# A fused linear-attention and MLP kernel: w_in products of batch 0 ahead of the last normalisation column, with the loads behind them reordered

## The chip, the cores and the metric

The kernel runs on one core of a Trainium2 chip. The metric is the device time of that core in microseconds, the median of several executions. The profile's span is mostly about 1.8 us shorter than that time. "Column c" below means one of the four 128-row slices of the MLP's input x.

Differences of a few tenths are therefore read in the profiles, and medians are only the check.

## The reference

Eight batches of 8 heads, 576 positions, head size 64. Each head's keys and values make a 64x64 matrix, the queries are multiplied by it, and the result is normalised over the head's 64 values. The heads side by side are the rows of an MLP with an ELU between its two matrices.

```python
kv  = np.einsum('bhsd,bhse->bhde', k, v)
out = np.einsum('bhsd,bhde->bhse', q, kv)
rms = np.sqrt(np.mean(out * out, axis=-1, keepdims=True) + 1e-06)
x   = (out / rms * g_norm).transpose(0, 2, 1, 3).reshape(4608, 512)
h   = x @ w_in                                   # 512 x 2048
g   = np.where(h > 0, h, np.exp(np.minimum(h, 0)) - 1)
return g @ w_out                                 # 2048 x 512
```

Inputs and output are fp32; the kernel multiplies in bf16.

## The kernel before

The work goes in nine groups of 512 rows: the first 512 positions of each batch, then one group of all the remainders. TensorE alternates between group T's w_in products (`mm1`), group T-1's w_out products (`mm2`) and the attention of T+1. Only the start differs: nothing has been loaded yet. Batch 0's attention is done with x transposed from the outset, one column c at a time, and TensorE is kept busy with products of zeros (`idle`).

```python
    packed_kv(0)
    for c in range(4):
        fetch_packed_kv("k", 0, slice(c, c + 1))
        # ...
        fetch_packed_kv("v", 0, slice(c, c + 1))
    for s in range(4):
        load_w_in(s)                    # 512 columns each, fp32 to bf16 on the way
    fetch_packed_q(1)
    packed_kv(1)
    for name in "kv":
        fetch_packed_kv(name, 1, slice(0, 2))
    load_w_out(0)                       # four of sixteen row blocks
    for name in "kv":
        fetch_packed_kv(name, 1, slice(2, 4))
    # ...
    fetch_q(0)                          # sync queue, two DMAs
    # ...
    exp_first(2)
    square_first(3, V)                  # copy and multiply on VectorE
    scale_first(1)
    scale_first(2)
    mean0[3] = bank(3)
    idle(idle_ps, 5)
    mean_first(3)
    log_first(3)
    exp_first(3)
    scale_first(3)                      # last column of x
    head.close()
    # ... PSUM pools: ps_at one tile of two banks, ps_m1 two such tiles, ps_m2 two banks
    for c in range(KC):                 # 16 products: tiles 0 to 3, column by column
        for f in (2, 3, 0, 1) if c == 0 else range(4):
            nc.tensor.matmul(firsts[f // 2][:, f % 2, :],
                lhsT=w_in_sb[:, c, f * P : f * P + P], rhs=x0[:, c, :],
                start=(c == 0), stop=(c == KC - 1))
    # ...
    for i in range(2):
        elu(0, i, [(0, 2, firsts[i])], i == 0)()
    for i in range(2, 8):
        mm1(0, i, relu=i in (2, 4, 7), spare=i in (3, 6))()
        if i in (3, 5):
            load_w_out(i // 2)
        if i == 5:
            at["q"]()                   # transposes of batch 1's Q
    # ... w_out 12 to 15, batch 2's loads ...
    at["kv0"]()                         # K1/V1 product, first half of the heads
    # ...
    for j in order:
        mm2_quarter(0, j, 0)            # w_out blocks 0 to 3
    at["kv1"]()
    at["se"]({0: None, 1: wide})        # Q1 times KV1, then squares, sums, scales
    # ...
    for j in order:
        mm2_quarter(0, j, 1)            # needs w_out blocks 4 to 7
    # ... blocks 8 to 15, with batch 1's x transposes x0 and x1 between them
```

Of the kernel before, what the change touches and what calls it, by code (L numbers as in the profile page):

```python
# [8 lines left out]
FP32 = mybir.dt.float32  # L9
# [7 lines left out]
def kernel(  # L17
# [117 lines left out]
    def load_w_in(s):  # L135
        cols = slice(s * 512, s * 512 + 512)
        nc.gpsimd.dma_start(  # L137
            out=w_in_sb[:, :, cols], in_=moe_w_in.rearrange("(c p) f -> p c f", p=P)[:, :, cols]
        )

    def load_w_out(s):
        fs = slice(4 * s, 4 * s + 4)
        nc.gpsimd.dma_start(
            out=w_out_sb[:, fs, :], in_=moe_w_out.rearrange("(c p) f -> p c f", p=P)[:, fs, :]
        )
# [7 lines left out]
    def q_tile(b):  # L153
        bf["q", b] = qkvp.tile([P, J, H, D], BF16, name="q_bf", tag="q")
        st = raw.pop(("q", b))
        if b < B:
            return st.rearrange("p (h j d) -> p j h d", h=H, j=J)
# [27 lines left out]
    def q_t_single(q_pk, qt_ps, p):  # L185
        for j in range(J):
            for l in range(2):
                nc.tensor.transpose(
                    qt_ps[l * 64 : l * 64 + 64, p, j * P : j * P + P],
# [3 lines left out]

    def q_t_mm(q_sb, qt_ps, p):
        for j in range(J):
            nc.tensor.transpose(
                qt_ps[:, p, j * P : j * P + P],
                q_sb[:, j, 2 * p : 2 * p + 2, :],
                ident,
            )  # L200
# [50 lines left out]
    def attention(T):  # L251
        st = {}

        def q_t():
# [3 lines left out]
            for p in range(NPAIR):  # L258
                q_t_single(raw["q", T], qt_ps, p)
# [130 lines left out]
    def mm1(T, i, cols=(slice(0, 512),), relu=False, spare=False, between=()):  # L390
# [4 lines left out]
        if spare:  # L395
            h_ps = [ps_m2.tile([P, G], FP32, name="h_ps", tag="mm2") for _ in range(2)]
            parts = [(a, a + 1, h_ps[a].rearrange("p (a t) -> p a t", a=1)) for a in range(2)]
        else:
            both = ps_m1.tile([P, 2, G], FP32, name="h_ps", tag="mm1")
# [91 lines left out]

    packed_kv(0)
# [5 lines left out]
    for s in range(4):  # L498
        load_w_in(s)
    fetch_packed_q(1)  # L500
    packed_kv(1)
    for name in "kv":
        fetch_packed_kv(name, 1, slice(0, 2))
    load_w_out(0)
# [11 lines left out]
    fetch_q(0)  # L516
# [14 lines left out]
    def idle(ps, n):  # L531
        for _ in range(n):
            nc.tensor.matmul(ps, lhsT=zeros[:, 0:P], rhs=zeros, start=True, stop=True)

    kv_ps = ps_head.tile([P, 2, G], FP32, name="kv_ps", tag="kv")
    idle_ps, qt_b, g_ps = bank(0), bank(1), bank(2)
    mean0 = {1: bank(3)}
    qt_ps = [
        t.bitcast(BF16).rearrange("p (r t) -> p r t", r=2) for t in (bank(4), bank(5), qt_b)
    ]  # L540
    idle(idle_ps, 9)
    q_st = q_tile(0)
    qT0 = attp.tile([P, NPAIR, G], BF16, name="qT", tag="qT")

    def q_cast(p, eng):
        hs = slice(2 * p, 2 * p + 2)
        copy_on(eng, bf["q", 0][:, :, hs, :], q_st[:, :, hs, :])

    for p, eng in ((0, V), (1, A)):
        q_cast(p, eng)  # L550
        q_t_mm(bf["q", 0], qt_ps[0], p)
    nc.vector.tensor_copy(out=qT0[:, 0:2, :], in_=qt_ps[0])
    idle(idle_ps, 2)
    for p, eng in ((2, V), (3, A)):
        q_cast(p, eng)
# [25 lines left out]
    def square_first(c, eng):  # L581
        if eng is A:
            nc.scalar.activation(sq0[c], se0[c], AF.Square)
        else:
            nc.vector.tensor_copy(out=r0[c], in_=se0[c])
            nc.vector.tensor_tensor(out=sq0[c], in0=r0[c], in1=se0[c], op=ALU.mult)
# [15 lines left out]
    q_t_mm(bf["q", 0][:, :, 4:8, :], qt_ps[1], 0)  # L602
    nc.vector.tensor_copy(out=qT0[:, 2, :], in_=qt_ps[1][:, 0, :])
    kv_first(0)
    q_t_mm(bf["q", 0][:, :, 4:8, :], qt_ps[2], 1)
    nc.scalar.copy(qT0[:, 3, :], qt_ps[2][:, 1, :])
# [8 lines left out]
    se0 = {c: bank(c) for c in range(2)}  # L615
    se_first(0)
    square_first(0, A)
    kv_first(1)
    idle_ps = bank(4)
    mean0[0] = bank(2)  # L620
    mean_first(0)
    log_first(0)
    se_first(1)
    square_first(1, A)
    exp_first(0)
    idle(idle_ps, 1)
    kv_first(2)
    idle(idle_ps, 1)
    mean_first(1)
    scale_first(0)  # L630
    for c in range(2, 4):
        se0[c] = bank(2 + c)
    se_first(2)
    square_first(2, A)
    log_first(1)
    exp_first(1)
    kv_first(3)
    idle_ps = bank(2)
# [227 lines left out]
```

## Time and profile before

| | before |
|---|---|
| median time | 285.86 us (3 runs), 285.78 with the three runs taken beside the changed kernel |
| span of the profile | 283.9 us |
| TensorE busy | 97% |
| first w_in product | 15.34 us |
| first product of batch 1 | 47.69 us |

The head of the page of the kernel before: span, the busy time of the engines with their shares of the span, and from the second part the rows of 40 equal slices (7.1 us each).

```profile
span 283.9 us, 5147 instructions
PE 274.1 (97%) x2115; PEld 129.6 (46%) x2145; DVE 161.2 (57%) x235; ACT 152.8 (54%) x217; POOL 53.1 (19%) x93
...
PE   7899999999999999999999999999999999999994
...
DMA  7999999797993596356953794355233123010122
GB/s 193 204 207 202 206 203 178 224 167 135 177 173 57 150 158 158 74 144 82 194 122 113 111 195 104 101 132 157 39 92 94 77 39 99 10 76 0 75 74 74
```

TensorE is the bound, and the loads run flat out for the first six slices, to about 43 us. Busy time of pipelined matmuls overstates, so the better reading is the distance between starts: a 128x512 product starts 0.216 us after the one ahead of it (eight take 1.73 us).

Next, lines of the timeline of TensorE of the kernel before. Columns: start in us, us until the last of the merged instructions ends, engine, line, operation, output<-inputs, partitions x elements, count, and in brackets the idle time ahead and what ended it. L533 are products of zeros, L589 and L665 the last mean and the first w_in products; L177, L212 and L453 are the K1/V1 product, Q1 times KV1, and the w_out products; L406 at the end is batch 1's first.

```profile
13.76 1.24 PE L533 MATMUL bank<-zeros 128*128 128x512 bf16 x5
15.12 0.39 PE L589 MATMUL bank<-sq,means 128*128 128x512 bf16 x1
15.34 0.38 PE L665 MATMUL at<-xT,w_in_sb 128*128 128x512 bf16 x1
...
30.37 0.48 PE L177 MATMUL at<-v_pk,k_pk 64*64 64x64 bf16 x36
31.01 3.63 PE L453 MATMUL o_ps<-w_out_sb,gT 128*128 128x512 bf16 x15 [0.17 <-DMA w_out_sb<-in_moe_w_out_dram]
34.57 0.48 PE L177 MATMUL at<-v_pk,k_pk 64*64 64x64 bf16 x36
35.43 0.41 PE L212 MATMUL at<-kv_sb,qT 64*128 64x64 bf16 x16 [0.38 <-ACT kv_sb L363]
...
36.44 5.34 PE L453 MATMUL o_ps<-w_out_sb,gT 128*128 128x512 bf16 x23 [0.37 <-DMA w_out_sb<-in_moe_w_out_dram]
...
47.69 2.54 PE L406 MATMUL h_ps<-xT,w_in_sb 128*128 128x512 bf16 x11
```

Three holes stand here: after the first K1/V1 product (0.64 us from start to start), after the second (0.86) and after Q1 times KV1 (1.01). Two of them end with a w_out load.

When a load lands can be read from GpSimd, whose queue lets it issue a new DMA only when an older one has landed. Lines of GpSimd's timeline of the kernel before:

```profile
14.85 0.74 POOL L143 DMA_DIRECT2D w_out_sb<-in_moe_w_out_dram  x1 [1.66 <-DMA w_in_sb<-in_moe_w_in_dram]
18.07 0.70 POOL L118 DMA_DIRECT2D k_pk<-in_k_dram  x1 [2.48 <-DMA w_in_sb<-in_moe_w_in_dram]
20.57 0.71 POOL L118 DMA_DIRECT2D v_pk<-in_v_dram  x1 [1.80 <-DMA w_in_sb<-in_moe_w_in_dram]
23.11 0.74 POOL L143 DMA_DIRECT2D w_out_sb<-in_moe_w_out_dram  x1 [1.83 <-DMA w_in_sb<-in_moe_w_in_dram]
```

The four w_in slices landed about 0.3 us ahead of these starts: 14.6, 17.8, 20.3 and 22.8 us.

### The profile page before, as it was taken

The numbers are of one execution on the slowest core, as the hardware profiler recorded it, in microseconds if no ns is written. First come the engines' busy times: TensorE is split into PE (matmuls) and PEld (weight loads), VectorE is DVE, ScalarE is ACT, GpSimd is POOL, SyncE is SP. The second block draws the span as 40 slices with busy tenths as digits, with TensorE's granted clock in tenths as the row PEclk, the third lists the DMA queues.
The fourth block names the chain that finished last, engine by engine and source line by source line (L and its number), as shares of the span: only waits on it lengthen the run. The fifth ranks groups of instructions, "written<-read, shape, count | busy, mean of one in ns | idle before, by whom it ended". The sixth has DMA issues, their size and how long they took to land.

```text
span 283.9 us, 5147 instructions
## 1 busy us (share of the span) xinstructions
PE 274.1 (97%) x2115; PEld 129.6 (46%) x2145; DVE 161.2 (57%) x235; ACT 152.8 (54%) x217; POOL 53.1 (19%) x93
## 2 busy tenths in 40 slices
PE   7899999999999999999999999999999999999994
PEld 2444454445444444444444444444444444444444
DVE  2458561779378646934694458544864486444400
ACT  2779544766496337633773378246923692333311
POOL 7834302341431241004210421002000000000000
PEclk9999999999999999999999999999999999999999
DMA  7999999797993596356953794355233123010122
GB/s 193 204 207 202 206 203 178 224 167 135 177 173 57 150 158 158 74 144 82 194 122 113 111 195 104 101 132 157 39 92 94 77 39 99 10 76 0 75 74 74
DMA packets 55963, 35.98 MB, mean 127 GB/s; under 512 B 32772, under 2 KB 53508, under 8 KB 55940
## 3 DMA queue, kind: packets, MB, share of 16 engines
q0 software_dynamic: 20192, 17.30, 39.7%
q1 hardware_dynamic: 35348, 17.83, 23.2%
q10 hardware_dynamic: 400, 0.52, 0.6%
q8 instruction: 16, 0.26, 0.4%
q14 instruction: 7, 0.06, 0.1%
HBM read 36.70 MB, written 9.44 MB: 163 GB/s over the span
## 4 chain that ended last, share of the span: by engine, by line
PE 80%; DMA 11%; DVE 4%; issue 1%; ACT 1%; POOL 1%; DVEq 0%; POOLq 0%
PE h_ps L406 36%; PE o_ps L453 36%; PE o_ps L825 5%; DMA w_in_sb<-in_moe_w_in_dram 5%; DMA w_out_sb<-in_moe_w_out_dram 5%; DMA k_pk<-in_k_dram 2%; PE at L177 1%; DVE gT L437 1%; DVE xs L240 1%; DVE ss L229 1%; POOL w_in_sb L137 1%; PE at L212 1%; PE se_ps L212 1%; DVE elu_e L429 0%; PE at L316 0%
## 5 line engine op out<-in xcount | busy, mean ns | idle before, releaser
L406 PE MATMUL h_ps<-xT,w_in_sb 128*128 128x512 bf16 x556 | 130.7, 379 | 0.3
L453 PE MATMUL o_ps<-w_out_sb,gT 128*128 128x512 bf16 x489 | 117.9, 379 | 1.8 <-DMA w_out_sb<-in_moe_w_out_dram 0.5
L418 ACT ACTIVATE elu_e<-h_ps 128x1024 bf16<-128x1024 f32 (+1 forms) x75 | 73.1, 982 | 82.6 <-PE h_ps L406 81.0
L406 PEld LDWEIGHTS <-w_in_sb 128*128 128x128 bf16 x560 | 53.2, 98 | 64.5 <-DVE xT L344 1.7
L453 PEld LDWEIGHTS <-gT 128*128 128x128 bf16 x512 | 49.8, 98 | 59.5 <-issue 0.3
L429 DVE TENSOR_SCALAR elu_e<-elu_e 128x1024 bf16<-128x1024 bf16 (+1 forms) x76 | 32.3, 425 | 75.4 <-ACT elu_e L418 75.4
L437 DVE TENSOR_TENSOR gT<-elu_e,h_ps 128x1024 bf16<-128x1024 bf16 (+1 forms) x56 | 64.1, 1145 | 5.8
L466 ACT COPY o_sb<-o_ps 128x512 f32<-128x512 f32 x32 | 18.5, 586 | 17.4 <-PE o_ps L453 17.4
L229 DVE TENSOR_REDUCE ss<-sq 128x16 f32<-128x1024 bf16 x16 | 19.3, 1217 | 7.7 <-ACT sq L224 6.9
L151 POOL COPY q_bf<-q_pk 128x512 bf16<-128x512 bf16 x24 | 14.9, 648 | 26.3 <-DMA q_pk<-in_q_dram 22.6
L424 ACT ACTIVATE elu_h<-h_ps 128x1024 bf16<-128x1024 f32 x19 | 19.3, 1015 | 0.0
L437 DVE TENSOR_TENSOR gT<-elu_e,elu_h 128x1024 bf16<-128x1024 bf16 x19 | 13.5, 713 | 3.6 <-ACT elu_h L424 2.4
L825 PE MATMUL o_ps<-w_out_sb,gT 128*128 128x512 bf16 (+1 forms) x79 | 14.0, 336 | 0.1
L125 POOL COPY gate<-qT 1x1 bf16<-1x1 bf16 x6 | 1.1, 179 | 61.5 <-DMA qT<-q_bf 61.5
L240 DVE TENSOR_TENSOR xs<-at,ss 128x512 bf16<-128x512 f32 x18 | 11.5, 681 | 1.2 <-ACT ss L236 1.2
L104 POOL DMA_DIRECT2D q_pk<-in_q_dram x14 | 10.6, 764 | 3.6 <-issue 1.9
L825 PEld LDWEIGHTS <-gT 128*128 128x128 bf16 x80 | 7.7, 98 | 6.4 <-DVE gT L437 0.4
L224 ACT ACTIVATE sq<-at 128x1024 bf16<-128x1024 f32 x9 | 9.4, 1044 | 1.5 <-PE at L212 1.5
L118 POOL DMA_DIRECT2D k_pk<-in_k_dram x12 | 8.4, 700 | 5.4 <-DMA w_in_sb<-in_moe_w_in_dram 2.5
L118 POOL DMA_DIRECT2D v_pk<-in_v_dram x12 | 8.5, 708 | 2.2 <-DMA w_in_sb<-in_moe_w_in_dram 1.8
L833 ACT COPY o_last<-o_ps 128x512 f32<-128x512 f32 (+1 forms) x5 | 2.5, 500 | 10.8 <-PE o_ps L825 10.8
L177 PEld LDWEIGHTS <-k_pk 64*64 64x64 bf16 x576 | 6.5, 107 | 3.8 <-issue 3.6
(71 smaller groups left out, 123.0 us busy)
## 6 DMA issues: line engine op xcount, KB each, us to landing
out_dram<-o_sb SPq DMA_DIRECT2D x16, 512.0 KB, 3.0
q_pk<-in_q_dram POOLq DMA_DIRECT2D x14, 256.0 KB, 5.3
k_pk<-in_k_dram POOLq DMA_DIRECT2D x6, 576.0 KB, 8.4
v_pk<-in_v_dram POOLq DMA_DIRECT2D x6, 576.0 KB, 11.5
w_in_sb<-in_moe_w_in_dram POOLq DMA_DIRECT2D x4, 512.0 KB, 10.6
w_out_sb<-in_moe_w_out_dram POOLq DMA_DIRECT2D x4, 512.0 KB, 15.3
st_q<-in_q_dram SPq DMA_DIRECT2D x2, 512.0 KB, 4.8
st_q<-in_q_dram SPq DMA_DIRECT2D x16, 64.0 KB, 2.5
```

The lines of the kernel that those rows point to most:

```text
L118: nc.gpsimd.dma_start(out=raw[name, b].rearrange("p h j d -> p h (j d)")[:, hs], in_=in_[:, hs])
L151: eng.tensor_copy(out=out_, in_=in_)
L229: nc.vector.reduce_sum(out=ss, in_=sq.rearrange("p c (h e) -> p (c h) e", h=H), axis=AX.X)
L240: nc.vector.tensor_tensor(out=xs.rearrange("p j (u l s e) -> p l j u s e", u=2, l=2, s=2)[:, l].rearrange("p j u s e -> p (j u) s e"), in0 ...
L406: nc.tensor.matmul(h_ps[a][:, cs], lhsT=w_in_sb[:, c, f * P : f * P + P], rhs=x(c, cs), start=(c == 0), stop=(c == KC - 1),)
L418: nc.scalar.activation(e[:, lo:hi, :], ps, AF.Exp)
L424: nc.scalar.activation(h[:, lo:hi, :], ps, AF.Relu)
L429: nc.vector.tensor_scalar(out=e[:, lo:hi, :], in0=e[:, lo:hi, :], scalar1=1.0, scalar2=1.0, op0=ALU.min, op1=ALU.subtract,)
L437: nc.vector.tensor_tensor(out=gT[T][:, 2 * i + lo : 2 * i + hi, :], in0=e[:, lo:hi, :], in1=h, op=ALU.add if relu else ALU.max,)
L453: nc.tensor.matmul(o_ps[T, j], lhsT=gT[T][:, f, j * P : j * P + P], rhs=w_out_sb[:, f, :], start=(f == 0), stop=(f == FC - 1),)
L466: nc.scalar.copy(o_sb[T][:, j % 2, :], o_ps.pop((T, j)))
L825: nc.tensor.matmul(ps, lhsT=gT[B][:, f, j * P : j * P + P], rhs=w_out_sb[:, f, cols], start=(f == 0), stop=(f == FC - 1),)
```

## The change

The intent is to start useful products earlier and to have each load when TensorE wants it. Six w_in output tiles are open at once (in banks that the head's pool still holds), and four products of column 0 run ahead of the last column's mean. ScalarE squares the last column. w_in comes in five slices, of which the second is narrow. The w_out loads go ahead of and between batch 1's, and TensorE's order after `mm1` follows. Batch 1's first four tiles run in two halves of 256 columns, so that they can begin when half of x is ready. "Q0 first on the sync queue" moves nothing: its two DMAs already stood first there, at 0.74 us.

```diff
-    for s in range(4):
-        load_w_in(s)
+    edges = (0, 512, 768, 1280, 1664, 2048)
+    for lo, hi in zip(edges, edges[1:]):
+        load_w_in(slice(lo, hi))
+    load_w_out(0, 4)
     fetch_packed_q(1)
+    load_w_out(4, 8)
     packed_kv(1)
     for name in "kv":
         fetch_packed_kv(name, 1, slice(0, 2))
-    load_w_out(0)
+    load_w_out(8, 10)
     for name in "kv":
         fetch_packed_kv(name, 1, slice(2, 4))
 ...
-    idle(idle_ps, 5)
+    pair = ps_head.tile([P, 2, G], FP32, name="h_ps", tag="kv")
+    products = {0: pair[:, 0, :], 1: pair[:, 1, :], 2: bank(6), 3: bank(7), 4: bank(0)}
+    first((0, 1, 2, 3), (0,))            # first(tiles, columns)
+    mean0[3] = bank(2)
     mean_first(3)
     log_first(3)
     exp_first(3)
     scale_first(3)
+    first((0, 1, 2, 3), (1,))
+    first((4,), (0, 1))
+    first((0, 1, 2, 3, 4), (2,))
+    products[5] = bank(1)
+    first((5,), (0, 1, 2))
+    first((0, 1, 2, 3, 4, 5), (3,))
 ...
-    at["kv0"]()
-    ...
     for j in order:
         mm2_quarter(0, j, 0)
+    at["q"]()
+    for j in order:
+        mm2_quarter(0, j, 1)
+    at["kv0"]()
+    for j in order[:3]:
+        mm2(0, j, 8, 10)
     at["kv1"]()
-    at["se"]({0: None, 1: wide})
+    mm2(0, order[3], 8, 10)
+    at["se"]({0: None, 1: ps_m1.tile([P, 2, G], FP32, name="se_ps", tag="mm1")})
 ...
     for j in order:
-        mm2_quarter(0, j, 1)
-    ...
+        mm2(0, j, 10, 12)
 ...
     for j in order:
         mm2(0, j, 12, FC, hold=j in (2, 3))
         if j == 3:
             mm2_out(0, 2)
             mm2_out(0, 3)
+        if j == 0:
+            at["x0"]()
+    at["x1"]()
 ...
+    for cs in (slice(0, 256), slice(256, G)):     # batch 1, tiles 0 to 3
+        for f in range(4):
+            for c in range(KC):
+                nc.tensor.matmul(firsts[f // 2][:, f % 2, cs], ...)
```

The cut parts: batch 0's attention on TensorE is resequenced with other banks, Q0's casts write one packed tile per head pair, and `mm1` gets a `home` for its PSUM tile in place of `spare`.

More of the change, by code (lines that the diff above doesn't have):

```diff
@@ L133, in unpack_q, with load_w_in @@
             copy_on(eng, bf["q", b][:, j], t[:, :, j])
-    def load_w_in(s):
-        cols = slice(s * 512, s * 512 + 512)
+    def load_w_in(cols):
         nc.gpsimd.dma_start(
@@ L139, in load_w_in, with load_w_out @@
         )
-    def load_w_out(s):
-        fs = slice(4 * s, 4 * s + 4)
+    def load_w_out(f0, f1):
+        fs = slice(f0, f1)
         nc.gpsimd.dma_start(
@@ L155, in q_tile @@
         st = raw.pop(("q", b))
-        if b < B:
-            return st.rearrange("p (h j d) -> p j h d", h=H, j=J)
         return st.rearrange("p (j h d) -> p j h d", h=H, j=J)
@@ L183, in kv_single, with q_t_single @@
                     )
-    def q_t_single(q_pk, qt_ps, p):
+    def q_t_single(q_pk, qt_ps, r, p):
         for j in range(J):
@@ L188, in q_t_single @@
                 nc.tensor.transpose(
-                    qt_ps[l * 64 : l * 64 + 64, p, j * P : j * P + P],
+                    qt_ps[l * 64 : l * 64 + 64, r, j * P : j * P + P],
                     q_pk[:, 2 * p + l, j, :],
@@ L192, in q_t_single @@
                 )
-    def q_t_mm(q_sb, qt_ps, p):
-        for j in range(J):
-            nc.tensor.transpose(
-                qt_ps[:, p, j * P : j * P + P],
-                q_sb[:, j, 2 * p : 2 * p + 2, :],
-                ident,
-            )
     def se_mm(T, h, qT, banks):
@@ L258, in q_t @@
             for p in range(NPAIR):
-                q_t_single(raw["q", T], qt_ps, p)
+                q_t_single(raw["q", T], qt_ps, p, p)
             nc.scalar.copy(qT[:, 0:2, :], qt_ps[:, 0:2, :])
@@ L388, with mm1 @@
     gT = {}
-    def mm1(T, i, cols=(slice(0, 512),), relu=False, spare=False, between=()):
+    def mm1(T, i, cols=(slice(0, 512),), relu=False, home="m1", between=()):
         if i == 0:
@@ L394, in mm1 @@
         x = xT[T]
-        if spare:
+        if home == "m2":
             h_ps = [ps_m2.tile([P, G], FP32, name="h_ps", tag="mm2") for _ in range(2)]
@@ L398, in mm1 @@
         else:
-            both = ps_m1.tile([P, 2, G], FP32, name="h_ps", tag="mm1")
+            if home == "at":
+                both = at_tile(FP32).rearrange("p (a t) -> p a t", a=2)
+            else:
+                both = ps_m1.tile([P, 2, G], FP32, name="h_ps", tag="mm1")
             h_ps = [both[:, a, :] for a in range(2)]
@@ L490 @@
     V, A, Q = nc.vector, nc.scalar, nc.gpsimd
+    fetch_q(0)
+    q_raw0 = raw.pop(("q", 0))
     packed_kv(0)
@@ L515 @@
     nc.vector.memset(one, 1.0)
-    fetch_q(0)
     g_row = const.tile([1, 2, D], FP32, name="g_row")
@@ L533, in idle, with cast_first, turn_first, turned @@
             nc.tensor.matmul(ps, lhsT=zeros[:, 0:P], rhs=zeros, start=True, stop=True)
+    bank(0), bank(1), bank(2), bank(3)
     kv_ps = ps_head.tile([P, 2, G], FP32, name="kv_ps", tag="kv")
-    idle_ps, qt_b, g_ps = bank(0), bank(1), bank(2)
-    mean0 = {1: bank(3)}
-    qt_ps = [
-        t.bitcast(BF16).rearrange("p (r t) -> p r t", r=2) for t in (bank(4), bank(5), qt_b)
-    ]
+    bank(6), bank(7)
+    idle_ps = bank(1)
     idle(idle_ps, 9)
-    q_st = q_tile(0)
+    q_st = q_raw0.rearrange("p (q h j d) -> p q j h d", q=4, h=2, j=J)
+    q_two = attp.tile([P, NPAIR, J, 2, D], BF16, name="q_two", tag="q_two", bufs=1)
     qT0 = attp.tile([P, NPAIR, G], BF16, name="qT", tag="qT")
-    def q_cast(p, eng):
-        hs = slice(2 * p, 2 * p + 2)
-        copy_on(eng, bf["q", 0][:, :, hs, :], q_st[:, :, hs, :])
-    for p, eng in ((0, V), (1, A)):
-        q_cast(p, eng)
-        q_t_mm(bf["q", 0], qt_ps[0], p)
-    nc.vector.tensor_copy(out=qT0[:, 0:2, :], in_=qt_ps[0])
-    idle(idle_ps, 2)
-    for p, eng in ((2, V), (3, A)):
-        q_cast(p, eng)
+    def cast_first(pair, eng):
+        copy_on(eng, q_two[:, pair], q_st[:, pair])
+    def turn_first(ps, pairs):
+        for r, pair in enumerate(pairs):
+            for j in range(J):
+                nc.tensor.transpose(ps[:, r, j * P : j * P + P], q_two[:, pair, j], ident)
+    def turned(n):
+        return bank(n).bitcast(BF16).rearrange("p (r t) -> p r t", r=2)
+    cast_first(0, V)
+    cast_first(1, A)
+    qt_ps = turned(3)
+    turn_first(qt_ps, (0, 1))
+    nc.vector.tensor_copy(out=qT0[:, 0:2], in_=qt_ps)
+    idle(idle_ps, 4)
+    cast_first(2, V)
+    cast_first(3, A)
     kv0 = attp.tile([P, 2, 2, D], BF16, name="kv0", tag="kv0", bufs=1)
@@ L579, in se_first, with square_first @@
             )
-    def square_first(c, eng):
-        if eng is A:
-            nc.scalar.activation(sq0[c], se0[c], AF.Square)
-        else:
-            nc.vector.tensor_copy(out=r0[c], in_=se0[c])
-            nc.vector.tensor_tensor(out=sq0[c], in0=r0[c], in1=se0[c], op=ALU.mult)
+    def square_first(c):
+        nc.scalar.activation(sq0[c], se0[c], AF.Square)
     def mean_first(c):
@@ L600, in scale_first, with first @@
         )
-    q_t_mm(bf["q", 0][:, :, 4:8, :], qt_ps[1], 0)
-    nc.vector.tensor_copy(out=qT0[:, 2, :], in_=qt_ps[1][:, 0, :])
-    kv_first(0)
-    q_t_mm(bf["q", 0][:, :, 4:8, :], qt_ps[2], 1)
-    nc.scalar.copy(qT0[:, 3, :], qt_ps[2][:, 1, :])
+    se0, mean0, products = {}, {}, {}
+    def first(fs, cs):
+        for c in cs:
+            for f in fs:
+                nc.tensor.matmul(
+                    products[f],
+                    lhsT=w_in_sb[:, c, f * P : f * P + P],
+                    rhs=x0[:, c, :],
+                    start=(c == 0),
+                    stop=(c == KC - 1),
+                )
+    qt_ps = turned(7)
+    turn_first(qt_ps, (2,))
+    nc.scalar.copy(qT0[:, 2, :], qt_ps[:, 0, :])
+    kv_first(0)
+    idle(idle_ps, 1)
+    se0[0] = bank(6)
+    se_first(0)
+    square_first(0)
+    qt_ps = turned(0)
+    turn_first(qt_ps, (3,))
+    nc.vector.tensor_copy(out=qT0[:, 3, :], in_=qt_ps[:, 0, :])
+    idle_ps = bank(3)
+    kv_first(1)
+    mean0[0] = bank(2)
+    mean_first(0)
+    log_first(0)
+    se0[1] = bank(7)
+    se_first(1)
+    square_first(1)
+    exp_first(0)
+    g_ps = bank(1)
     nc.tensor.matmul(
@@ L614 @@
     nc.vector.tensor_copy(out=g_col, in_=g_ps[:, 0:1])
-    se0 = {c: bank(c) for c in range(2)}
-    se_first(0)
-    square_first(0, A)
-    kv_first(1)
-    idle_ps = bank(4)
-    mean0[0] = bank(2)
-    mean_first(0)
-    log_first(0)
-    se_first(1)
-    square_first(1, A)
-    exp_first(0)
-    idle(idle_ps, 1)
-    kv_first(2)
-    idle(idle_ps, 1)
-    mean_first(1)
-    scale_first(0)
-    for c in range(2, 4):
-        se0[c] = bank(2 + c)
-    se_first(2)
-    square_first(2, A)
+    kv_first(2)
+    idle(idle_ps, 2)
+    se0[2] = bank(1)
+    se_first(2)
+    square_first(2)
+    mean0[1] = bank(0)
+    mean_first(1)
     log_first(1)
     exp_first(1)
+    idle(idle_ps, 1)
     kv_first(3)
-    idle_ps = bank(2)
+    scale_first(0)
     idle(idle_ps, 1)
-    mean_b = ps_head.tile([P, 2, G], FP32, name="mean_ps", tag="kv")
-    mean0[2] = mean_b[:, 0, :]
-    se_first(3)
+    mean0[2] = bank(2)
     mean_first(2)
     log_first(2)
+    se0[3] = bank(3)
+    se_first(3)
+    square_first(3)
     exp_first(2)
-    square_first(3, V)
+    idle(bank(0), 2)
     scale_first(1)
     scale_first(2)
-    mean0[3] = bank(3)
-    idle(idle_ps, 5)
+    pair = ps_head.tile([P, 2, G], FP32, name="h_ps", tag="kv")
+    products = {0: pair[:, 0, :], 1: pair[:, 1, :], 2: bank(6), 3: bank(7), 4: bank(0)}
+    first((0, 1, 2, 3), (0,))
+    mean0[3] = bank(2)
     mean_first(3)
@@ L654 @@
     scale_first(3)
+    first((0, 1, 2, 3), (1,))
[4 more added lines that the diff above has]
+    first((0, 1, 2, 3, 4, 5), (3,))
+    gT[0] = mlpg.tile([P, FC, G], BF16, name="gT", tag="gT")
+    single = [
+        [(a, a + 1, products[2 * i + a].rearrange("p (a t) -> p a t", a=1)) for a in range(2)]
+        for i in (1, 2)
+    ]
+    for i, parts in enumerate([[(0, 2, pair)]] + single):
+        elu(0, i, parts, i == 1)()
     head.close()
@@ L658 @@
     ps_m2 = ctx.enter_context(tc.tile_pool(name="ps_m2", bufs=2, space=bass.MemoryType.PSUM, reuse_waits="tile"))
-    gT[0] = mlpg.tile([P, FC, G], BF16, name="gT", tag="gT")
-    firsts = [ps_m1.tile([P, 2, G], FP32, name="h_ps", tag="mm1")]
-    firsts.append(at_tile(FP32).rearrange("p (a t) -> p a t", a=2))
-    for c in range(KC):
-        for f in (2, 3, 0, 1) if c == 0 else range(4):
-            nc.tensor.matmul(
-                firsts[f // 2][:, f % 2, :],
-                lhsT=w_in_sb[:, c, f * P : f * P + P],
-                rhs=x0[:, c, :],
-                start=(c == 0),
-                stop=(c == KC - 1),
-            )
-    at, ahead = attention(1), attention(2)
-    for i in range(2):
-        elu(0, i, [(0, 2, firsts[i])], i == 0)()
-    for i in range(2, 8):
-        mm1(0, i, relu=i in (2, 4, 7), spare=i in (3, 6))()
-        if i in (3, 5):
-            load_w_out(i // 2)
-        if i == 5:
-            at["q"]()
+    at, ahead = attention(1), attention(2)
+    for i in range(3, 8):
+        mm1(0, i, relu=i in (3, 5, 7), home={5: "m2", 6: "at"}.get(i, "m1"))()
     nc.gpsimd.tensor_copy(
@@ L683 @@
     )
-    load_w_out(3)
+    load_w_out(10, 12)
+    load_w_out(12, FC)
     fetch_packed_q(2)
@@ L688 @@
         fetch_packed_kv(name, 2)
-    at["kv0"]()
     both = ps_m1.tile([P, 2, G], FP32, name="o_ps", tag="mm1")
-    wide = ps_m1.tile([P, 2, G], FP32, name="se_ps", tag="mm1")
     for a in range(2):
@@ L706 @@
     for j in order:
-        mm2_quarter(0, j, 1)
-    for j in order[:2]:
-        mm2_quarter(0, j, 2)
-    at["x0"]()
-    for j in order[2:]:
-        mm2_quarter(0, j, 2)
-    at["x1"]()
+        mm2(0, j, 10, 12)
     unpack_q(2, Q)
@@ L779 @@
     ahead["qd"]()
+    gT[1] = mlpg.tile([P, FC, G], BF16, name="gT", tag="gT")
+    firsts = [ps_m1.tile([P, 2, G], FP32, name="h_ps", tag="mm1") for _ in range(2)]
+    for cs in (slice(0, 256), slice(256, G)):
+        for f in range(4):
+            for c in range(KC):
+                nc.tensor.matmul(
+                    firsts[f // 2][:, f % 2, cs],
+                    lhsT=w_in_sb[:, c, f * P : f * P + P],
+                    rhs=xT[1](c, cs),
+                    start=(c == 0),
+                    stop=(c == KC - 1),
+                )
     for i in range(8):
-        rest = mm1(1, i, relu=i in (1, 4), spare=i in (2, 5))
-        rest()
+        if i < 2:
+            elu(1, i, [(0, 2, firsts[i])], i == 0)()
+        else:
+            mm1(1, i, relu=i == 4, home="m2" if i in (2, 5) else "m1")()
         if i == 3:
```

## The prediction

> **What bounds the kernel now.** TensorE. The profile's first part has it busy 97% of 283.9 us. The timeline shows 128x512 matmuls following each other every 0.216 us (eight in 1.73 us in the chain of waits). From the first w_in product (15.34 us) on, the starts of successive matmuls leave few holes: about 1.1 us between 30 and 37 us (first w_out slice, the K1/V1 product and its copy, second w_out slice), and about 0.7 us between 72 and 92 us. So only the first 48 us can change.
>
> Those are ruled by the loads. The DMA row moves about 205 GB/s (counted in bf16) without a hole up to 45 us, and GpSimd's waits, with 0.3 us taken off, place the landings: w_in's first slice about 14.6 us, its last 22.8, w_out's first 30.8, its second 36.4. Products cannot start before 14.6 us. The timeline shows Q0 already first on the sync queue at 0.74 us, so that part of the change moves nothing.
>
> **What the change does.**
> 1. Filler to work: before, five idle matmuls wait for the square of head pair 3 (two DVE operations, 0.69 us each, ending 15.06 us). Afterwards ScalarE does it (0.60 us) and four c=0 products run before the last mean. I expect the first product at 14.65 us rather than 15.34. One mean (0.216 us) now lies inside the products: net gain 0.5 us. By an estimate from the ScalarE durations (0.60 to 0.69 us) the last x0 column comes at 18.05 us, 0.4 later than before, but 18 products cover it up to 18.7.
> 2. Loads: the bytes are the same, the order new. At 0.2 MB/us I estimate w_out 0-3 at 25.5, Q1 28.1, w_out 4-7 at 30.7, the K1/V1 halves at 33.7 and 38, the last w_out at 42 us. The new TensorE order needs each later than that. So the 1.1 us of holes mostly go. The 256-column slice has 512-byte rows; the Trainium skill, DMA: Bandwidth & Descriptors, Specifications, gives 512 B as the least for line rate, so I expect no loss; no run here shows it yet.
> 3. Costs: six tiles end together, so their ELU queues on ScalarE (exp 1.02 us a pair) and DVE (max from PSUM 1.22 us); the fifth pair of products waits about 0.35 us for its PSUM banks. Attention 1's normalisation took 4.5 us before its transposes; 20 matmuls cover 4.3. In batch 1 the first four products run in two 256-column halves: at the last line's 0.115 us each (32 in 3.67 us) this costs 0.2 us, and both pairs end together, so ELU starts some 1.9 us later; I allow 0.4 us of PSUM waits there.
>
> **Sum.** -0.5 - 1.1 + 0.35 + 0.15 + 0.2 + 0.4 = -0.5 us. All of it is on TensorE's chain, and after 92 us nothing changes. Predicted 285.3 us, 80% range 284.2 to 286.2. Chances: faster by over 2% 0.01, within 2% 0.98, slower by over 2% 0.01.
>
> **What would show it.** Right: the first w_in product at 14.6 to 14.8 us; TensorE's waits for w_out gone; the 1.1 us of holes between 30 and 37 us under 0.5; batch 1's first product 0.7 to 1.2 us earlier than 47.69; a stretch from there to 92 us longer by 0.3 to 0.7 us. Wrong: products starting at 15.2 or later; a wait for DMA between 20 and 45 us.
>
> **What would make it wrong.** The second w_in slice landing after 17 us, or the deeper queue slowing the first slice; the six-tile ELU backlog delaying the whole of batch 0; or no bank waits at all in batch 1, which would give 284.5.

## More of the kernel before

The kernel before shows some executions up to 287.8 us with a mean TensorE clock of 0.987 instead of 1.0.

Together they are 1.13 us.

## The result and the profile after

| | before | after |
|---|---|---|
| median of 6 runs | 285.78 us | 285.72 us |
| ratio, 95% interval | | 0.9996 (0.9983 to 1.0009) |
| first w_in product | 15.34 us | 14.49 us |
| first product of batch 1 | 47.69 us | 47.74 us |

A ratio here is the mean time of one kernel's runs over that of the other's of the same rounds, so it is not quite the ratio of the medians. The time is the same. The useful products start 0.85 us earlier, the 1.13 us of holes are gone, and yet batch 1 starts 0.05 us later. So about two microseconds were gained and given back between 14 and 48 us.

Head of the page of the changed kernel, then its TensorE timeline for the two places that matter. L607 are the 24 products of the six tiles, L398 the next ones, L174 and L201 the K1/V1 and Q1 products, L305 the transposes of batch 1's x, L803 batch 1's first products in halves.

```profile
span 284.1 us, 5184 instructions
PE 275.6 (97%) x2131; PEld 131.0 (46%) x2162; DVE 159.2 (56%) x231; ACT 153.1 (54%) x221; POOL 54.8 (19%) x95
```

```profile
14.49 0.60 PE L607 MATMUL h_ps<-xT,w_in_sb 128*128 128x512 bf16 x2
...
16.01 0.59 PE L607 MATMUL bank<-xT,w_in_sb 128*128 128x512 bf16 x2
16.91 0.61 PE L607 MATMUL bank<-xT,w_in_sb 128*128 128x512 bf16 x2 [0.30 <-DMA w_in_sb<-in_moe_w_in_dram]
...
20.37 1.89 PE L398 MATMUL h_ps<-xT,w_in_sb 128*128 128x512 bf16 x8
22.57 0.81 PE L398 MATMUL h_ps<-xT,w_in_sb 128*128 128x512 bf16 x3 [0.31 <-DVE gT L429]
...
37.59 0.48 PE L174 MATMUL at<-v_pk,k_pk 64*64 64x64 bf16 x36
38.00 1.25 PE L445 MATMUL o_ps<-w_out_sb,gT 128*128 128x512 bf16 x5
39.40 0.48 PE L174 MATMUL at<-v_pk,k_pk 64*64 64x64 bf16 x36
39.81 0.60 PE L445 MATMUL o_ps<-w_out_sb,gT 128*128 128x512 bf16 x2
40.35 0.41 PE L201 MATMUL at<-kv_sb,qT 64*128 64x64 bf16 x16
...
45.45 0.62 PE L305 MATMUL at<-ident,xs 128*128 128x128 bf16 x8
45.91 1.03 PE L445 MATMUL o_ps<-w_out_sb,gT 128*128 128x512 bf16 x4
47.30 0.61 PE L305 MATMUL at<-ident,xs 128*128 128x128 bf16 x8 [0.37 <-ACT xT L312]
47.74 3.66 PE L803 MATMUL h_ps<-xT,w_in_sb 128*128 128x256 bf16 x32
```

Four matmuls that should start 0.22 us after the one ahead start later. The two matmuls at 16.01 end their turn at 16.45, and the next starts at 16.91: 0.46 us for the second w_in slice. The eight at 20.37 would be done at 22.10, and the next starts at 22.57: 0.47 us until VectorE has read the PSUM tile of the first pair. The first transposes come 0.20 us late, for VectorE's scaling, and the second 0.53 us late, behind ScalarE's copy of the first transposes. (The bracketed times are counted from the modelled end of the matmul, so they are shorter than these start-to-start ones.)

The ledger from the first product to batch 1, in us, read from starts in the two traces:

| term | predicted | measured |
|---|---|---|
| first product earlier | -0.69 | -0.85 |
| last mean now among the products | +0.22 | +0.22 |
| holes at 30 to 37 us gone | -1.1 | -1.13 |
| wait for the second w_in slice | 0 | +0.46 |
| wait for the first pair's PSUM banks | +0.35 | +0.47 |
| first x transposes late | +0.15 | +0.20 |
| second x transposes late | 0 | +0.53 |
| one more switch to narrow products before Q1 times KV1 | 0 | +0.10 |
| batch 1: halves (to its K/V product) | +0.6 | +0.04 |
| sum | -0.47 | +0.04 |

Read directly, the changed kernel is 0.05 us later at batch 1's first product and 0.09 us at its K2/V2 product, so 0.05 us are left that no term names.

From batch 1's K2/V2 product on, the two TensorE timelines run 0.1 us apart or less.

### The profile page after: what moved, and what is told of

Same layout as the page of the kernel before. It is cut to its first block, busy times and chain, and to the rows that moved or that the text cites. A ratio compares the mean times of both kernels' runs of the same rounds, so it can differ in the third digit from the quotient of the medians.

```text
span 284.1 us, 5184 instructions
## 1 busy us (share of the span) xinstructions
PE 275.6 (97%) x2131; PEld 131.0 (46%) x2162; DVE 159.2 (56%) x231; ACT 153.1 (54%) x221; POOL 54.8 (19%) x95
## 4 chain that ended last, share of the span: by engine, by line
PE 88%; ACT 4%; DVE 3%; DMA 2%; issue 1%; another core or an unknown queue 1%; SPq 0%; DVEq 0%
PE h_ps L398 39%; PE o_ps L445 36%; PE o_ps L857 5%; DMA st_q<-in_q_dram 2%; PE at L174 2%; PE h_ps L803 1%; DVE ss L218 1%; PE at L201 1%; ACT elu_e L410 1%; ACT sq L213 1%; PE at L398 1%; PE bank L577 1%; PE bank L529 1%; ACT o_sb L458 1%
## 5 line engine op out<-in xcount | busy, mean ns | idle before, releaser
L398 PE MATMUL h_ps<-xT,w_in_sb 128*128 128x512 bf16 x524 | 123.7, 379 | 0.5 <-DVE gT L429 0.3
L410 ACT ACTIVATE elu_e<-h_ps 128x1024 bf16<-128x1024 f32 (+1 forms) x72 | 70.9, 996 | 84.3 <-PE h_ps L398 78.9
L398 PEld LDWEIGHTS <-w_in_sb 128*128 128x128 bf16 x536 | 50.9, 98 | 62.0 <-DVE xT L333 1.7
L429 DVE TENSOR_TENSOR gT<-elu_e,h_ps 128x1024 bf16<-128x1024 bf16 (+1 forms) x53 | 62.6, 1181 | 5.9 <-DVE elu_e L421 0.5
L416 ACT ACTIVATE elu_h<-h_ps 128x1024 bf16<-128x1024 f32 (+1 forms) x19 | 18.5, 989 | 0.0
L529 PE MATMUL bank<-zeros 128*128 128x512 bf16 x19 | 7.3, 508 | 1.4 <-DVE zeros L506 1.2
```

The costliest lines, as they stand in the source:

```text
L398: nc.tensor.matmul(h_ps[a][:, cs], lhsT=w_in_sb[:, c, f * P : f * P + P], rhs=x(c, cs), start=(c == 0), stop=(c == KC - 1),)
L410: nc.scalar.activation(e[:, lo:hi, :], ps, AF.Exp)
L416: nc.scalar.activation(h[:, lo:hi, :], ps, AF.Relu)
L429: nc.vector.tensor_tensor(out=gT[T][:, 2 * i + lo : 2 * i + hi, :], in0=e[:, lo:hi, :], in1=h, op=ALU.add if relu else ALU.max,)
```

## The experiments

Theory: TensorE is one chain in the first 48 us, each wait above is a separate term of its sum, and taking one away gives that time back at the end. Rival: the arrival of the loads and the normalisation of batch 1 fix the end of batch 0, so that whatever is won earlier turns into a later wait.

Each group of four ran on one chip beside the kernel before, whose medians there were 285.73, 285.69 and 285.77 us. The changed kernel was not run again beside them, so a difference to it goes by way of the kernel before. All runs lie within 2% of the kernel before; what is read here are tenths of a microsecond.

| run | median us | ratio to before (95%) | first product of batch 1, us |
|---|---|---|---|
| changed kernel | 285.72 | 0.9996 (0.9983 to 1.0009) | 47.74 |
| e1_order | 284.94 | 0.9962 (0.9940 to 0.9985) | 46.75 |
| e2_four_slices | 287.46 | 1.0054 (1.0027 to 1.0082) | 48.69 |
| e3_old_loads | 288.63 | 1.0092 (1.0066 to 1.0118) | 50.47 |
| e4_x1_bank | 285.26 | 0.9974 (0.9953 to 0.9994) | 47.19 |
| e5_early_kv | 286.25 | 1.0015 (0.9999 to 1.0031) | 47.80 |
| e6_order_kv | 285.57 | 0.9991 (0.9975 to 1.0008) | 47.20 |
| e7_whole | 286.78 | 1.0031 (1.0007 to 1.0055) | 48.88 |
| e8_before_loads | 288.78 | 1.0105 (1.0084 to 1.0126) | 50.60 |
| e9_order_x1 | 284.87 | 0.9965 (0.9948 to 0.9983) | 46.40 |
| e10_kv_copies | 285.54 | 0.9987 (0.9972 to 1.0003) | 47.35 |
| e11_all | 285.07 | 0.9975 (0.9958 to 0.9992) | 46.59 |
| e12_mean_first | 286.30 | 1.0017 (0.9999 to 1.0034) | 47.88 |

All gave correct results. Twelve kernels ran.

### e1_order: another order of the first 24 products

```diff
-    first((0, 1, 2, 3), (1,))
-    first((4,), (0, 1))
-    first((0, 1, 2, 3, 4), (2,))
+    first((0, 1, 2, 3), (1, 2))
+    first((4,), (0, 1, 2))
+    first((0, 1, 2, 3), (3,))
     products[5] = bank(1)
     first((5,), (0, 1, 2))
-    first((0, 1, 2, 3, 4, 5), (3,))
+    first((4, 5), (3,))
```

> Changed kernel with only the order of the first 24 w_in products altered: the third column's products of tiles 0 to 3 run before tile 4 (so nothing waits for the second w_in slice, which landed at 16.85 us), and tiles 0 to 3 get their last column before tile 5 starts (so the ELU of tiles 0 and 1 starts about 1.05 us earlier). Theory (each wait on TensorE in the first 48 us is a separate term of the sum): the 0.46 us and 0.47 us waits at 16.2 and 21.9 us go, batch 1's first product comes at 46.9 instead of 47.74 us, and the time falls by 0.84 us to about 284.9. Rival (loads and the normalisation chain fix the end of batch 0, so what is won early turns into a later wait): batch 1 still starts near 47.7 us and the time stays at 285.7.

TensorE's timeline of this run; the numbers to compare are 16.91, 20.37, 22.57 and 47.74 above.

```profile
14.34 0.60 PE L607 MATMUL h_ps<-xT,w_in_sb 128*128 128x512 bf16 x2
...
19.84 5.34 PE L398 MATMUL h_ps<-xT,w_in_sb 128*128 128x512 bf16 x24
...
46.75 3.66 PE L803 MATMUL h_ps<-xT,w_in_sb 128*128 128x256 bf16 x32
```

Both waits are gone: tile 6 starts at 19.84 us and 24 products follow without a break. Batch 1 starts 0.99 us earlier (0.15 of it because the first slice happened to land earlier in this run), and the median falls by 0.78 us, as the theory said (the slowest execution, 285.10 us, lies below the changed kernel's fastest, 285.69). The rival fails here: 0.46 and 0.47 us were lost to nothing but the order of 24 products. By the time that the second slice lands, the third column of x is ready, so there was other work to put in front of tile 4. (A wait of 0.10 us for that column is new.)

### e2_four_slices: w_in in four equal slices

```diff
-    edges = (0, 512, 768, 1280, 1664, 2048)
+    edges = (0, 512, 1024, 1536, 2048)
```

> Changed kernel with w_in in four equal slices of 512 columns as before. Theory: the second slice then lands near 17.8 us as in the kernel before, tile 4's first product waits until then instead of 16.9 us, everything behind it in order is 0.9 us later, time about 286.6. Rival (the narrow slice is no gain because landing does not follow its size): first product of tile 4 still at 16.9 to 17.1 us, time 285.7.

TensorE's timeline of this run:

```profile
17.85 0.61 PE L607 MATMUL bank<-xT,w_in_sb 128*128 128x512 bf16 x2 [1.26 <-DMA w_in_sb<-in_moe_w_in_dram]
```

In the profile, tile 4 starts at 17.85 instead of 16.91 us, and batch 1 0.95 us later: as expected. The median rose by 1.74 us, more than the 0.9 expected; the profiled execution (287.16 us) was the fastest of four, and 0.22 us of its rise lie in batch 1 at about 59 us (see e12). The rest is not explained by the one profile: the changed kernel's profiled execution lay 0.19 us above its median, and that of e2 0.30 us below its own. The narrow slice is worth having, but it landed at 16.9 us and not at the 16 us that its bytes suggested.

### e3_old_loads and e8_before_loads: the load order alone, both ways

e3 is the changed kernel with the old order behind w_in:

```diff
-    load_w_out(0, 4)
     fetch_packed_q(1)
-    load_w_out(4, 8)
     packed_kv(1)
     for name in "kv":
         fetch_packed_kv(name, 1, slice(0, 2))
-    load_w_out(8, 10)
+    load_w_out(0, 4)
     for name in "kv":
         fetch_packed_kv(name, 1, slice(2, 4))
+    load_w_out(4, 8)
+    load_w_out(8, 10)
```

> Changed kernel with the load order of before behind w_in (Q1, half of K1/V1, w_out 0 to 3, the other half, w_out 4 to 7), five w_in slices kept. Theory: w_out 0 to 3 lands near 31.1 instead of 25.6 us and the first w_out product waits for it (29.47 to 31.1, 1.6 us); w_out 4 to 7 lands near 36.7 where about 35.7 is needed, 1.0 us more; time about 288.3. Rival (load order is worth no more than the 0.5 us of w_out waits that the profile of before shows): time at most 286.3.

e8 is the kernel before with the new load order (the same lines the other way round, and w_out 10 to 15 behind `mm1`):

> The kernel before with nothing changed but the order of the loads behind w_in (that of the changed kernel, w_in still in four slices). Theory (the load order pays only with the new TensorE order): the first K1/V1 half lands near 33.6 us and its product, wanted at 30.4, waits about 3 us; the 0.5 us of w_out waits go; time about 288.4. Rival (earlier w_out is a gain by itself): 285.3.

Longest entries of the view of what TensorE waited for, first e3, then e8 (us in total, times, longest):

```profile
PE o_ps L445 <- DMA w_out_sb<-in_moe_w_out_dram: 2.6, 2, 1.8
```

```profile
PE at L188 <- DMA q_pk<-in_q_dram: 1.9, 2, 1.2
PE at L177 <- DMA v_pk<-in_v_dram: 1.3, 1, 1.3
```

e3 waits 2.6 us for w_out and takes 2.9 us longer than the changed kernel. e8 takes 3.1 us longer than the kernel before; the sum was right and its parts were not. I had expected 3 us at K1/V1, but Q1, which I had forgotten, waits first (1.9 us) and V1 then only 1.3. In these traces the loads run as one stream, at 193 to 207 KB per us for the first 43 us in the kernel before: what one gets earlier another gets later. Neither order is better by itself; each fits one order of TensorE's work. A profile that shows 0.5 us of w_out waits does not say that moving w_out costs or gains 0.5.

### e4_x1_bank: the second transposes in a tile of their own

```diff
-    at["x1"]()
+    at["x1"](ps_m1.tile([P, 2, G], FP32, name="xt_ps", tag="mm1")[:, 0, :])
```

> Changed kernel with the second half of attention 1's transposes written to a PSUM tile of its own, not to the second half of the tile from which ScalarE is still reading the first half. Theory: the 0.53 us wait of those transposes (46.77 to 47.30 us) for ScalarE's copy is a wait for the shared tile; they start at 46.8, and batch 1's first product, which itself needs that copy at 47.25, starts at 47.3 instead of 47.74; time 285.3. Rival (the transposes wait for something else, such as their own scaled rows): no change, 285.7.

TensorE's timeline of this run:

```profile
45.80 1.03 PE L445 MATMUL o_ps<-w_out_sb,gT 128*128 128x512 bf16 x4
46.66 0.61 PE L305 MATMUL xt_ps<-ident,xs 128*128 128x128 bf16 x8
47.19 3.70 PE L803 MATMUL h_ps<-xT,w_in_sb 128*128 128x256 bf16 x32
```

The transposes follow at once, batch 1 starts 0.55 us earlier (0.11 of it because the w_in slices landed earlier in this run), and the median falls by 0.46 us. In the changed kernel TensorE waited to write the second half of a two-bank tile until ScalarE had read the first half. The Trainium skill (PSUM — Partial Sum Buffer, Specifications) gives a bank as 2 KiB per partition; each half holds 1024 bf16 values, so the halves lie in different banks, and the page's rule on bank collisions asks for a guard by bank and quadrant. So the program guarded more than the page asks. The runs show only that a tile of its own takes the wait away.

### e5_early_kv, e10_kv_copies, e6_order_kv: the K1/V1 products earlier

```diff
-    for j in order:
+    for j in order[:3]:
         mm2_quarter(0, j, 1)
     at["kv0"]()
-    for j in order[:3]:
-        mm2(0, j, 8, 10)
+    mm2_quarter(0, order[3], 1)
+    mm2(0, order[0], 8, 10)
     at["kv1"]()
-    mm2(0, order[3], 8, 10)
+    mm2(0, order[1], 8, 10)
     at["se"](...)                        # then mm2(0, j, 8, 10) for the other two
 ...
-        if j == 3:
-            mm2_out(0, 2)
-            mm2_out(0, 3)
-        if j == 0:
-            at["x0"]()
+        if j in (2, 3):                  # e10: both copies at j == 3, as before the edit
+            mm2_out(0, j)
+        if j == 3:
+            at["x0"]()
```

> Changed kernel (product order as changed) with the K1/V1 products moved up behind 12 and 18 of the w_out products, so that attention 1's products with Q start about 0.85 us earlier (39.5 instead of 40.35 us), and with its first transposes one group of w_out products earlier, so that 28 instead of 24 w_out products and both transposes fill the 6.9 us of normalisation behind them. The K1/V1 second half landed near 37.8 us, so the loads permit it. Theory (the waits of 0.2 and 0.5 us before batch 1 come from a normalisation chain that starts too late): both go, batch 1's first product at 47.0 instead of 47.74 us, time about 285.0. Rival (ScalarE's output copies, queued before the x copy, set the time): first product still after 47.5 us, 285.5 or more.

This missed, through an edit of mine. Q1 times KV1 did start 1.0 us earlier (39.36 us, 0.12 of it from earlier landings), but a new wait stood behind it. Its TensorE timeline and, in the second fence, ScalarE's at that time:

```profile
39.93 3.63 PE L445 MATMUL o_ps<-w_out_sb,gT 128*128 128x512 bf16 x16
44.33 1.02 PE L445 MATMUL o_ps<-w_out_sb,gT 128*128 128x512 bf16 x3 [0.77 <-ACT o_sb L458]
```

```profile
43.71 0.57 ACT L458 COPY o_sb<-o_ps 128x512 f32<-128x512 f32 x1
```

I had moved the copy of output block 2 ahead of block 3's last products. The two blocks are the halves of one PSUM tile, and TensorE does not write the second half until ScalarE's copy of the first ends at 44.28 us. It is the wait of e4 in another place. e6 (this edit with e1's order) carries the same wait, so its expectation of 284.2 could not be met:

> The product order that took 0.8 us off and the earlier K1/V1 products together. Theory (separate terms that add): batch 1's first product at 46.1 to 46.2 us, with about 0.3 us of new wait for the K1/V1 second half (landing near 37.8 us where 37.5 is wanted), time about 284.2. Rival (the second gain shares its cause with the first, or the loads now bind: last w_out slice landing at 41.6 us): no better than the product order alone, 284.9.

It took 285.57 us, 0.68 us less than e5, so the product order was worth about the same on this kernel as in e1. e10 repeats e5 with both copies behind block 3:

> The earlier K1/V1 products again, but with both output copies on ScalarE after the second w_out group has ended, as in the changed kernel, and not one of them between the two groups, which share one PSUM tile. Theory (the 0.8 us wait in that run was TensorE waiting to write one half of a tile while ScalarE read the other half, the same thing as the 0.5 us wait of the second transposes): that wait goes, batch 1's first product at 47.2 instead of 47.80 us, time 285.2. Rival (the wait came from ScalarE being busy with the normalisation): it stays, or moves to the copies behind, 286.2.

The wait is gone, the first product of batch 1 came at 47.35 us (47.2 expected; its wait for the second w_in slice was 0.14 us longer than in the changed kernel's profile), and the median fell by 0.71 us against e5. It is only 0.18 us below the changed kernel's, where 0.5 was expected, and its interval does not exclude 1: the K1/V1 move by itself buys little.

### e7_whole: batch 1's first tiles in whole columns

```diff
-    for cs in (slice(0, 256), slice(256, G)):
+    for cs in (slice(0, G),):
```

> Changed kernel with the first four products of batch 1 in whole 512 columns, as before. Theory (the halves cost 0.05 us on the chip, and hide the second half of x, which is ready at 48.8 us): first product at 48.8 instead of 47.74 us, time 286.7. Rival (the prediction's: the halves cost 0.2 us of matmul rate and 0.4 us of waits for PSUM): the 1.05 us later start is won back by 0.6 us, time 286.2.

The view of TensorE's waits of this run has a new first entry, for VectorE's scaling of the second half of x:

```profile
PE h_ps L803 <- DVE xT L314: 0.9, 1, 0.9
```

Batch 1 starts at 48.88 us, and from there to its K2/V2 product e7 needs 7.00 us, the changed kernel 7.04 and the kernel before 7.00. So the halves cost 0.04 us, not the 0.6 of the prediction, and hide 1.1 us of waiting that the change's own late normalisation causes. 32 products of 256 columns took 3.50 us, 0.109 us each.

### e12_mean_first: the head start undone

```diff
-    first((0, 1, 2, 3), (0,))
     mean0[3] = bank(2)
     mean_first(3)
+    first((0, 1, 2, 3), (0,))
```

> Changed kernel with the four first-column products moved back behind the last mean (the head start undone, all else kept). Theory (the second w_in slice eats the head start in the changed kernel's order): first product at 15.4 instead of 14.5 us, but tile 4's wait at 16.9 us goes, so the 24 products end only about 0.2 us later and the time rises by 0.2 us to 285.9. Rival (the head start counts in full): 286.6.

TensorE's timeline of this run, its first product:

```profile
15.32 0.59 PE L607 MATMUL h_ps<-xT,w_in_sb 128*128 128x512 bf16 x2
```

The first product comes 0.83 us later and batch 1 only 0.14 us later (47.88): in the changed kernel's order the wait for the second slice eats nearly all of the head start. That is what the theory said. The time, however, rose by 0.58 us, between the 0.2 of the theory and the 0.9 of the rival, so that the median alone does not decide. The profiled execution was 0.40 us longer than the changed kernel's, and 0.24 us of it stand at 59 us, in batch 1, where a product starts late; the PSUM tile that it writes is the one that VectorE has just read. Lines of the timeline at that time, GpSimd's DMA issues and one VectorE operation, of e12 first and then of the changed kernel:

```profile
56.21 1.49 POOL L104 DMA_DIRECT2D q_pk<-in_q_dram  x2 [0.33 <-POOL gate L125]
...
57.25 0.70 DVE L421 TENSOR_SCALAR elu_e<-elu_e 128x1024 bf16<-128x1024 bf16 x1
```

```profile
56.18 1.66 POOL L104 DMA_DIRECT2D q_pk<-in_q_dram  x2 [0.33 <-POOL gate L125]
...
57.12 0.42 DVE L421 TENSOR_SCALAR elu_e<-elu_e 128x1024 bf16<-128x1024 bf16 x1
```

The same VectorE operation took 0.70 us in one and 0.42 in the other, while GpSimd was issuing DMAs. The Trainium skill (SBUF — State Buffer, Who interferes with whom) says that VectorE in a 2-port mode and GpSimd take one shared port pair in turn, whole instruction by whole instruction, and that issue order decides who waits. The two traces agree: where VectorE took 0.28 us longer, the DMA issues took 0.17 us less. In the kernel before, VectorE had read that tile by 57.66 us, about 1.2 us ahead of need (an estimate from the 0.216 us of the products between); with the halves it is done at 58.86 us, so that such a collision now costs time.

### e9_order_x1 and e11_all: together

> The product order (worth 0.8 us alone) and the second transposes in a PSUM tile of their own (0.45 us alone) together. Theory (two separate waits on the one chain): they add; batch 1's first product at 46.3 instead of 47.74 us, time 284.4 to 284.5. Rival (one of them only moves the wait on): at best the better of the two alone, 284.9.

> Product order, second transposes in their own tile, and the earlier K1/V1 products with the copies put right. Theory: after the first two changes only about 0.25 us of wait is left before batch 1, and the earlier K1/V1 products buy it with 0.45 us of wait for V1's second half (landing near 37.8 us), so no better than the first two: batch 1's first product at 46.3 to 46.5 us, 284.4 to 284.7. Rival (the normalisation chain still binds): first product at 46.0, 284.1.

e9 is e1's and e4's edits, e11 those with e10's. In its profile e9 starts batch 1 at 46.40 us, 1.34 us before the changed kernel, and the profiled execution took 284.42 us: the expected value. But the median is 284.87, hardly below e1 alone, and the executions spread from 284.42 to 285.51. So the two gains add up to 48 us, and the end of the program keeps the second only in some executions. e11's profiled execution (285.43 us, against its median of 285.07) shows what can take it. Lines of the timeline of e11 (GpSimd's copies, two VectorE operations and the TensorE product that comes late), then the first three of e9:

```profile
81.47 1.91 POOL L150 COPY q_bf<-q_pk 128x512 bf16<-128x512 bf16 x3 [3.47 <-DMA q_pk<-in_q_dram]
...
82.15 0.77 DVE L421 TENSOR_SCALAR elu_e<-elu_e 128x1024 bf16<-128x1024 bf16 x1
...
83.02 0.91 DVE L429 TENSOR_TENSOR gT<-elu_e,elu_h 128x1024 bf16<-128x1024 bf16 x1
...
91.67 1.67 PE L398 MATMUL h_ps<-xT,w_in_sb 128*128 128x512 bf16 x7 [0.65 <-DVE gT L429]
```

```profile
80.11 1.72 POOL L150 COPY q_bf<-q_pk 128x512 bf16<-128x512 bf16 x3 [2.94 <-DMA q_pk<-in_q_dram]
...
81.86 0.42 DVE L421 TENSOR_SCALAR elu_e<-elu_e 128x1024 bf16<-128x1024 bf16 x1
...
82.38 0.69 DVE L429 TENSOR_TENSOR gT<-elu_e,elu_h 128x1024 bf16<-128x1024 bf16 x1
```

GpSimd's three copies start when a load lands. In e11 they fall on two VectorE operations, which take 0.57 us longer together; at 90.9 us TensorE then waits 0.8 us for VectorE, where the other profiles show 0.2 to 0.3. In e9's profile the copies end before those operations begin. A stretch by itself is not enough: in e8's profile two VectorE operations at 81 and 82 us, earlier in their group's work, took as long (0.85 and 0.91 us), and TensorE's wait later on was 0.2 us. That this is what separates e9's slower executions from its fastest is an inference: they left no profile. e11 is no better than e9, as the theory expected.

## Why the prediction was right, and where it was not

The prediction (285.3 us, 284.2 to 286.2, the same within 2%) holds the measured 285.72. The mechanism held less well than the number. Of the marks by which it was to be known, the first product, the vanished w_out waits and the holes came true. Two did not: batch 1's first product was to come 0.7 to 1.2 us earlier and came 0.05 later, and the stretch from there to 92 us was to be 0.3 to 0.7 us longer and grew by no more than 0.04. Point by point:

- **First product at 14.65 us.** Right: 14.49. The first w_in slice is the floor, and TensorE sits right behind it.
- **The 1.1 us of holes go.** Right: 1.13 us, and there is no wait for w_out between 20 and 45 us in the changed kernel. e3 and e8 show that load order and TensorE order do this together only.
- **"18 products cover it".** Half right. "It" is the last column of x: that was ready at 17.91 us, and its products came at 19.07. What failed is that the 18 products were to run without a break up to 18.7, so that the sum has no term for the second w_in slice. The ninth of them, tile 4's first, needs that slice. By the prediction's own start and 0.216 us for each of eight products and a mean it was due at 16.6 us (an estimate), so the 17 us that the prediction named as its limit for this slice was already too late. In the trace it was due at 16.45 and started at 16.91: 0.46 us were lost (e1, e2).
- **Why the slice was late.** I had reckoned with its bytes alone, which at 0.2 MB per us lead to about 16 us. Each of these loads raises its semaphore (the signal that others wait for) 16 times, and the packed trace keeps the times. Of the second slice's 16, 15 had come by 15.84 us, as the bytes say, and the last came at 16.86. The kernel before shows the same: 15 by 17.08 us and the last at 17.79, which is the step of 3.2 us against 2.5. So only the last of the 16 signals was late, not the stream (the third point of the list at the end says what goes with it).
- **"the fifth pair of products waits about 0.35 us for its PSUM banks".** Right in kind, 0.47 us measured. e1 shows that it was not the price of six tiles but of finishing all six together.
- **x of batch 1.** The 0.15 us before the first transposes measured 0.20. The 0.53 us before the second were not foreseen: a wait on a shared tile, shown by e4 and, by accident, by e5 against e10.
- **Halves of batch 1, 0.2 + 0.4 us.** Failed by size: 0.04 us (e7). The rate was 0.109 us and not 0.115 (32 products in 3.67 us in the timeline's merged line, which counts the modelled end of the last one), and the backlog of ELU fell into a reserve on VectorE that I had not looked at.

So two waits that were missed (about 1.0 us) stood against one cost that was too large by 0.56. That these cancelled in part, under a range of 2 us, is luck: the gain of 0.5 us that the sum promised is nowhere in the timelines at batch 1, though the medians alone (an interval of about -0.5 to +0.3 us) could hardly tell. What stays open is why e2 lost 1.74 us where its profile shows 1.2, and which executions of e9 lose 0.4 us after 48 us.

The experiments lead to a better kernel than both: e1's reordered products give 0.9962 of the time before (median 284.94 us), and with the separate tile of e4 0.9965 (284.87 us). Both intervals lie below 1, and which of the two is faster is not settled.

## What to carry to other kernels

When the stage ahead of a full pipeline is shortened, list every wait that the new order can have, not only those that the old one had, and look for work that is already ready to put in front of each: here 24 products in another order were worth more than the whole change. Finish the first accumulations early instead of all together, because the engines behind them need a start. A tile that two engines use in halves can make one wait for the other's half: give the halves tiles of their own, or keep reads of one away from writes of the other. And where a product stands close behind a load, look at when the load's last part comes, not only at its bytes: here the last part came a microsecond late.

## What the Trainium skill lacked or had wrong

- TensorE: Matmul & The Clock Gate, Back-to-back issue gap: it gives about 131 ns per 512-column matmul in a stream of weight load and matmul pairs. The streams read here run at 216 ns (eight in 1.73 us), which is what the page's other formula for an isolated gap gives; 256 columns took 109 ns.
- DMA: Bandwidth & Descriptors, Specifications: 512 B as the least for line rate agrees nearly. In the changed kernel's packet records, microseconds of nearly only 512-byte packets moved 189 to 192 KiB, those of only 1024-byte ones 202 to 205.
- No page that I found says that a load's landing can miss its bytes by this much: a slice of half the size landed 2.4 us after the one ahead, where 1.3 us of bytes lay between. Runtime: NRT & Kernel Launch, Instruction fetch mechanics, where it would belong, tells of 16 KiB instruction fetches but not of what they do to loads. In all 14 traces a 16 KiB fetch of 0.94 to 0.98 us starts between 14.2 and 14.9 us. In the load that lands next the last of the 16 semaphore raises comes 0.7 to 1.2 us after the fifteenth, and the lag stays in the loads behind it; in the load ahead of the fetch it was at most 0.14. After the next such fetch (31.9 us in the kernel before, 34.3 to 37.2 in the others) the fifteenth falls behind the fourteenth too, by 0.7 to 1.1 us, against at most 0.14 ahead of it. So the delay goes with the fetch wherever the fetch lies, as if it held up one DMA engine. No run moved a fetch on purpose, and the records do not say which engine carried it, so the cause is not shown.
- SBUF — State Buffer, Who interferes with whom: its account of the shared port pair agrees with e11 (0.77 against 0.42 us) and e12 (0.70 against 0.42). It could add that the moment of collision can hang on when a load lands, as GpSimd's copies do in e11 and e9. That one program differs between its executions for this reason was not seen.
